# Retention and a token/channel mixer on one core: first-front tiles in either group of PSUM banks, and k of two batches cast unscaled by the DMA queue

## The chip, the cores and the metric

The kernel runs on one core of a Trainium2 chip. The metric is the device time of one execution in microseconds (us). The core has TensorE (PE in the profile; its weight loads are a row of their own, PEld), VectorE (DVE), ScalarE (ACT), GpSimd (POOL) and SyncE (SP). Transfers are issued by SP and by POOL; in this kernel those that change the data type on the way are issued by POOL. Matrix products land in PSUM, of which the kernel uses eight banks of 128 x 512 numbers of 32 bits.

## The reference

Inputs q, k, v have the shape (4 batches, 8 heads, 768 steps, 64). The first half is retention with a decay for each head, the second a mixer over the 768 steps and then over the 512 channels:

```
gamma = 1.0 - 2.0 ** (-5.0 - np.arange(H))
for t in range(S):
    state = gamma * state + einsum('bhd,bhe->bhde', k[:, :, t], v[:, :, t])
    y[:, :, t] = einsum('bhd,bhde->bhe', q[:, :, t], state) / sqrt(D)
x  = y with the heads laid side by side                      # (4, 768, 512)
h  = relu(x^T @ w_tok1) @ w_tok2                             # tokens: 768 -> 256 -> 768
u  = x + h^T
out = u + relu(u @ w_ch1) @ w_ch2                            # channels: 512 -> 1536 -> 512
```

All inputs and the output are of 32 bits; the products are made from operands of 16 bits (f16).

## The kernel before, in words

**Tiling.** The 768 steps are cut into six chunks of 128 and the eight heads into four pairs. For each batch there is a `front` of four pairs (`front(b, p)`: retention and token mixing) and a `back` (`back(b)`: channel mixing). Within a chunk retention is a masked product of scores with v; between chunks it is a state per head, carried with the decay to the power 128.

**The decay.** `gk` holds the decay to the minus step for each head, a number for each partition; `gy` the matching factor of the output. Line 317 multiplies k by `gk` while it turns it from f32 into f16 (`k16`, two VectorE instructions for a pair). Everything that uses k, the scores as well as the states, uses this scaled tile.

**One pair of a front, in order.** Loads of k (into `kf`, 32 bits, line 261), q (line 283 in batch 0, 280 in batch 1) and v (line 286). In batches 0 and 1 POOL issues them, and q and v are cast to f16 on the way; only the k of batch 0's pair 0 comes by SP. Batches 2 and 3 come by SP as 32 bits, and POOL casts q and v (line 298). Then: the scaling (317); the transposes of k and q on TensorE into a PSUM tile (333 and 337) and their copies out (345, VectorE for k and ScalarE for q in batch 0, ScalarE for both in batch 1), while batches 2 and 3 turn k and q by transposing transfers of SP (352); the sums of k and v of each chunk (366) and the running states `U` (375, 378), copied to `r` by ScalarE (385) and VectorE (392); the scores (408); their mask (421 on VectorE, or, for six tiles of batch 0 named in `ASIDE`, a plain copy by ScalarE at 419 and a cut by POOL at 425); the output y (442, 445), scaled into x (456, 460, 473); then the token mixing: product with w_tok1 (496), relu (504), product with w_tok2 (517), addition to x (524), f16 copy (535) and the turn of u into `uT` (548 and 557 in batch 0, a transfer of SP at 571 later).

**Back.** `ch1` (line 604) multiplies `uT` by w_ch1, 12 tiles for each half of the steps, with relu at 617; `ch2` (637) multiplies by w_ch2, adds x (646), and SP stores (653).

**PSUM.** Each temporary is a `Slot` with a tag; `BUFS` says how many buffers a tag has. The eight banks are `fa=5` for the fronts and `ba=3` for the backs; in batch 0 the token mixing of pairs 0 and 1 (`TOKBA = 2`) uses `ba` too.

**Order.** The program of each engine is written out in the order that a planner (`arrange`) finds. Every step is an `Op` with its engine, a rank (`prio`), the time for which it holds its engine (`occ`), a latency, its dependences and the slots that it takes and uses. The planner keeps a clock for each engine, lets a slot be taken when the users of the buffer's last holder have ended, and picks the step that can start first, by rank within 20 ns. Transfers have modelled durations on two rings, SP's and POOL's. POOL's transfers of batches 0 and 1 and of the weights are chained in one order (`queue`): for pair p of batch 0 k, q, v, then behind pair 3 w_tok1, w_tok2 (line 207) and w_ch1 in two pieces, then batch 1, with w_ch2 behind its pair 1. While batch 0's front has gaps, TensorE is given products with zeros (line 198), as many as the planned gap holds.

Of the kernel before, what the change touches and what calls it, by code (L numbers as in the profile page):

```python
# [13 lines left out]
ALU = mybir.AluOpType  # L14
# [3 lines left out]
def kernel(  # L18
# [11 lines left out]
    nc = tc.nc  # L30
# [53 lines left out]
    for t in r16:  # L84
# [8 lines left out]

    BUFS = dict(kf=4, qf=4, vf=4, k16=3, q16=4, v16=4, kT=4, qT=4, U=3, am=8, x16=2, h1=4, u16=3, u16w=2,
                x=3, uT=3, h2=2, o=3, r16=NR, fa=5, ba=3)
    SEM, GUARD = 80, 100
    EARLY, LATE, DIRECT = 1000, 12, 3
    LONG, XK, XQ, XU, XBAR = 1, 2, 2, 1, 1200
    RING = dict(SP=3, POOL=6)
    QLONG = 1200  # L100
    ASIDE, RACT = ((1, 1), (1, 3), (2, 1), (2, 3), (3, 1), (3, 3)), ()
    KPOOL = ()
    FILL, TOKBA, PRE, TWICE, SOFT = 0.75, 2, 2, 1, 2
    ops = []

    class Slot:


        def __init__(self, tag):
            self.tag, self.users, self.tile = tag, [], None  # L110

# [11 lines left out]
    def arrange():  # L123


        way = {}
        for op in reversed(ops):
            if op.first is not None:
                way[op] = way.get(op, 0) + op.lat + SEM
                for d in op.deps:  # L130
                    way[d] = max(way.get(d, 0), way[op])
        for op in ops:
            if op.first is not None:
                op.prio = (op.prio[0], 0, EARLY * op.first - way[op], op.first)
        free = dict(PE=5700, ACT=5000, DVE=4600, POOL=1100, SP=1300, SPring=1300, POOLring=1300)
        taken = {t: [] for t in BUFS}
        todo, order, ring = list(ops), [], dict(SP=[], POOL=[])
        while todo:
            best = []
            for op in todo:  # L140
                if any(d.end is None for d in op.deps):
                    continue
                start = free[op.eng]
                if op.dma and len(ring[op.eng]) >= RING[op.eng]:
                    start = max(start, ring[op.eng][op.count - 1 - RING[op.eng]])
                for d in op.deps:
                    if d.eng == op.eng and (d.dma or d.eng == "PE"):
                        continue
                    start = max(start, d.end + (30 if d.eng == op.eng else SEM) + op.guard)
                more = {}  # L150
                for s in op.takes:
                    q = taken[s.tag]
                    n = len(q) + more.get(s.tag, 0) - BUFS[s.tag]
                    more[s.tag] = more.get(s.tag, 0) + 1
                    if n >= 0:
                        old = q[n]
                        if any(u.end is None for u in old.users):
                            break
                        start = max([start] + [u.end + SEM for u in old.users])
                else:  # L160
                    best.append((start, op))
            t = min(b[0] for b in best)

            eng = min(best, key=lambda b: (b[0], b[1].prio))[1].eng
            start, op = min((b for b in best if b[1].eng == eng and b[0] <= t + 20),
                            key=lambda b: b[1].prio)
            free[op.eng] = start + op.occ
            op.start = start
            if op.dma:

                mine, other = op.eng + "ring", ("POOL" if op.eng == "SP" else "SP") + "ring"
                at = max(free[mine], start + (op.occ + 200 if op.eng == "POOL" else 50))
                both = max(0, free[other] - at)
                shared = min(op.dma, both // 2)
                if op.eng == "SP" and at > 5000:

                    at, shared = max(at, free[other]), 0
                free[mine] = at + op.dma + shared
                free[other] += shared
                op.end = free[mine] + 1600  # L180
                ring[op.eng] += [op.end if op.eng == "POOL" else free[mine]] * op.count
            else:
                op.end = start + op.lat
            for s in op.takes:
                taken[s.tag].append(s)
            todo.remove(op)
            order.append(op)
        return order
# [33 lines left out]
    def front(b, p):  # L222
        first = b == 0
        g = 0 if first else GUARD
        n = [0]

# [18 lines left out]
        srcs = dict(k=(k, Slot("kf")), q=(q, Slot("qf")), v=(v, Slot("vf")))  # L245
        KF = srcs["k"][1]

# [25 lines left out]
        def cast(slot, nm):  # L273
# [51 lines left out]
        def turn(src, dst, dep, eng):  # L325
            T = Slot("fa")

            def emit():
                T.tile = tp = tile_of(T, ps, [P, 512], FP).bitcast(F16)
                for c in range(NC):  # L330
                    if src is Q and soft and b < LONG:
                        for j in range(2):
                            nc.tensor.transpose(tp[j * D:(j + 1) * D, c * P:(c + 1) * P],
                                                src.tile[:, j * NC + c], ident16)
                        continue
                    o = src.tile[:, c] if src is K else src.tile[:, 2 * c:2 * c + 2]
                    nc.tensor.transpose(tp[:, c * P:(c + 1) * P], o.rearrange("p h d -> p (h d)"), ident16)  # L337
# [11 lines left out]
        def crossbar(src, dst, dep):  # L349
# [48 lines left out]
        for hf in range(2):  # L398
            A = [Slot("fa"), Slot("fa")]

# [10 lines left out]
            for j in range(2):  # L411
                off = first and (p, 2 * hf + j) in ASIDE
                M = AM[2 * hf + j]

                def emit(j=j, A=A, off=off, M=M):
# [16 lines left out]
        for hf in range(2):  # L432
            Y = Slot("fa")

# [53 lines left out]

        FA = "ba" if first and p < TOKBA else "fa"
        T1, H1 = Slot(FA), Slot("h1")  # L490

# [15 lines left out]
        wide = b >= XU  # L507
        T, UW = Slot(FA), Slot("u16w")
        for hf in range(2):
            T2, U16 = Slot(FA), UW if wide else Slot("u16")  # L510

# [28 lines left out]
            if first:  # L540
                T = Slot(FA)

# [168 lines left out]
```

## Time and profile before

| | |
|---|---|
| runs of the kernel before, median of 4 | 202.25 us (201.62 to 203.26) |
| the profiled execution | 201.41 us |
| its span in the profile | 199.7 us |
| granted TensorE clock | 0.998 |
| stand-in products, line 198, "fa" / "ba" | 37 and 3 instructions, 10.8 and 0.8 us |
| queue 0 (POOL's), packets and bytes | 25248, 9.83 MB |
| k loads issued by POOL | 7, 384.0 KB each, median 9.0 us to landing |
| v loads issued by POOL | 8, 192.0 KB each, median 7.4 us to landing |

The profile is one execution. A row of a chain or of a timeline begins with its start and its length in us, then engine, tile and line; a row of groups gives the busy time, the mean of one instruction in ns, and the idle time in front of it with what ended it. Of a transfer the answers give the time from the start of its issue to its landing. KB counts the bytes of the destination. The matrix products are pipelined, so that TensorE's busy share is not its share of peak. Time in which an engine that is not the bound stands idle costs nothing.

### The profile page before, as it was taken

The page shows a single profiled execution, that of the slowest core. Times are in us where ns is not written, and L with a number is a line of the kernel's source. Part 1 is how long each engine was busy: PE and PEld are TensorE (multiplying, and loading weights), DVE is VectorE, ACT ScalarE, POOL GpSimd, SP SyncE. Part 2 cuts the span into 40 slices and gives each one's busy share as a digit, 9 for nine tenths or more (in the row PEclk, how much of TensorE's full clock was granted, in tenths as well). Part 3 has the DMA queues.
Part 4 walks back from the last instruction along what each step waited for, and adds up shares of the span by engine and source line. Part 5 has one row for each costly group of instructions (what it writes and reads, how often), then busy time and mean ns, then how long its engine had stood idle before and what let it go on. Part 6 is the DMA issues. An engine that isn't in the chain of part 4 may idle for free.

```text
span 199.7 us, 4693 instructions
## 1 busy us (share of the span) xinstructions
PE 190.9 (96%) x1876; PEld 117.3 (59%) x1876; DVE 112.2 (56%) x285; ACT 92.3 (46%) x207; POOL 77.3 (39%) x124
## 2 busy tenths in 40 slices
PE   7698999999999999899999999999999999999993
PEld 2454796667766555666566755665666545545552
DVE  6599766585479675755786387628772021021021
ACT  7265996886682111275216530563326405504600
POOL 7997899944603531233534333343131000000000
PEclk9999999999999999999999999999999999999999
DMA  7999999999999989999999998999614021012012
GB/s 116 182 216 185 208 226 196 153 186 213 158 137 221 222 187 138 253 268 150 220 211 266 247 193 201 233 234 176 96 54 116 18 88 70 3 53 105 0 53 105
DMA packets 90069, 31.75 MB, mean 159 GB/s; under 512 B 82592, under 2 KB 85920, under 8 KB 90048
## 3 DMA queue, kind: packets, MB, share of 16 engines
q1 hardware_dynamic: 64800, 21.63, 55.8%
q0 software_dynamic: 25248, 9.83, 42.7%
q8 instruction: 14, 0.23, 0.5%
q14 instruction: 7, 0.06, 0.1%
HBM read 26.74 MB, written 6.29 MB: 165 GB/s over the span
## 4 chain that ended last, share of the span: by engine, by line
PE 79%; DMA 9%; POOL 6%; DVE 2%; issue 1%; SPq 1%; POOLq 0%; DVEq 0%
PE ba L637 30%; PE ba L604 28%; DMA wt<-in_moe_w_tok_dram 5%; PE fa L496 4%; PE fa L517 4%; PE fa L408 3%; DMA vf<-in_v_dram 3%; PE fa L445 2%; POOL v L286 2%; PE fa L442 2%; POOL kf L261 2%; PE fa L366 2%; PE fa L337 1%; DMA qT<-q 1%; POOL q L283 1%
## 5 line engine op out<-in xcount | busy, mean ns | idle before, releaser
L604 PE MATMUL ba<-uT,wc 128*128 128x384 f16 x384 | 69.2, 326 | 0.0
L637 PE MATMUL ba<-wc,h 128*128 128x512 f16 (+1 forms) x300 | 68.1, 371 | 0.0
L617 ACT ACTIVATE h<-ba 128x384 f16<-128x384 f32 x96 | 46.8, 492 | 38.4 <-PE ba L604 37.9
L604 PEld LDWEIGHTS <-wc 128*128 128x128 f16 x384 | 35.4, 98 | 22.1
L637 PEld LDWEIGHTS <-h 128*128 128x128 f16 x300 | 27.6, 98 | 25.8
L646 DVE TENSOR_TENSOR o<-x,ba 128x512 f32<-128x512 f32 (+1 forms) x25 | 16.6, 663 | 41.0 <-PE ba L637 41.0
L421 DVE TENSOR_TENSOR am<-fa,mask 128x384 f16<-128x384 f32 x58 | 30.0, 550 | 3.4 <-PE fa L408 2.8
L473 POOL CAST x<-x 128x384 f16<-128x384 f32 x30 | 15.2, 511 | 29.2 <-issue 19.3
L456 ACT ACTIVATE x<-fa,gy 128x192 f32<-128x192 f32 (+1 forms) x42 | 15.0, 424 | 15.7 <-PE fa L445 15.7
L524 DVE TENSOR_TENSOR x<-x,fa 128x384 f32<-128x384 f32 x28 | 14.7, 550 | 12.3 <-PE fa L517 12.1
L535 POOL CAST u16w<-x 128x384 f16<-128x384 f32 x24 | 11.9, 507 | 24.0 <-DVE x L524 23.7
L378 DVE SCALAR_TENSOR_TENSOR U<-U,gp,fa 128x64 f32<-128x64 f32 x64 | 17.7, 277 | 1.3
L317 DVE TENSOR_SCALAR k<-kf,gk 128x384 f16<-128x384 f32 x32 | 13.7, 470 | 4.5 <-DMA kf<-in_k_dram 4.5
L385 ACT ACTIVATE r<-U 64x320 f16<-64x320 f32 x16 | 7.5, 466 | 16.9 <-DVE U L378 16.9
L504 ACT ACTIVATE h<-fa 128x256 f16<-128x256 f32 x14 | 5.4, 386 | 20.8 <-PE fa L496 20.8
L445 PEld LDWEIGHTS <-am 128*128 128x128 f16 x192 | 12.2, 98 | 2.9
L445 PE MATMUL fa<-v,am 128*128 128x64 f16 x192 | 13.6, 193 | 0.0
L517 PEld LDWEIGHTS <-wt 128*128 128x128 f16 x192 | 11.9, 98 | 2.6 <-issue 0.2
L198 PE MATMUL fa<-zero 128*128 128x512 f16 x37 | 10.8, 428 | 2.5 <-DVE zero L52 1.3
L496 PEld LDWEIGHTS <-wt 128*128 128x128 f16 x192 | 11.7, 98 | 2.4 <-DMA wt<-in_moe_w_tok_dram 0.4
L442 PE MATMUL fa<-r,qT 128*128 128x128 f16 x80 | 12.1, 220 | 0.0
L517 PE MATMUL fa<-h,wt 128*128 128x128 f16 x168 | 12.0, 219 | 0.0
(61 smaller groups left out, 171.1 us busy)
## 6 DMA issues: line engine op xcount, KB each, us to landing
out_dram<-o SPq DMA_DIRECT2D x23, 256.0 KB, 2.6
kf<-in_k_dram SPq DMA_DIRECT2D x9, 384.0 KB, 5.2
qf<-in_q_dram SPq DMA_DIRECT2D x8, 384.0 KB, 5.2
vf<-in_v_dram SPq DMA_DIRECT2D x8, 384.0 KB, 5.5
kf<-in_k_dram POOLq DMA_DIRECT2D x7, 384.0 KB, 9.0
v<-in_v_dram POOLq DMA_DIRECT2D x8, 192.0 KB, 7.4
wc<-in_moe_w_ch_dram POOLq DMA_DIRECT2D x1, 1536.0 KB, 13.3
wc<-in_moe_w_ch_dram POOLq DMA_DIRECT2D x1, 1024.0 KB, 13.6
```

Source lines behind the costliest of these rows:

```text
L378: nc.vector.scalar_tensor_tensor(U[:, c], U[:, c - 1], gp[:, p:p + 1], o, ALU.mult, ALU.add)
L421: nc.vector.tensor_tensor(am, src[:, :HC], mask, ALU.mult)
L442: nc.tensor.matmul(o, QT.tile[:, c * P:(c + 1) * P], R[:, c - 1], start=True, stop=False)
L445: nc.tensor.matmul(o[:, j * D:(j + 1) * D], AM[2 * hf + j].tile[:, i], V.tile[:, j * NC + c], start=(c == 0), stop=(c == 0 or j == 1))
L456: nc.scalar.mul(dst[:, :, j * D:(j + 1) * D], yv[:, :, j * D:(j + 1) * D], gy[:, h:h + 1])
L473: nc.gpsimd.tensor_copy(X16.tile[:, half(hf)], X.tile[:, half(hf), pc])
L496: nc.tensor.matmul(acc[:, jt * P:(jt + 1) * P], wt1[:, i, jt * P:(jt + 1) * P], X16.tile[:, i], start=(i == 0), stop=(i == NC - 1))
L517: nc.tensor.matmul(acc[:, i * P:(i + 1) * P], wt2[:, jt, t], H1.tile[:, jt], start=(jt == 0), stop=(jt == NJ - 1))
L604: nc.tensor.matmul(acc[:, :SH], w[:, ct, f * P:(f + 1) * P], UT.tile[:, ct, sh * SH:(sh + 1) * SH], start=(ct == 0), stop=(ct == NP - 1))
L617: nc.scalar.activation(H2.tile[:, ft], A.tile[:, :SH], AF.Relu)
L637: nc.tensor.matmul(A.tile[:, :CW], H2.tile[:, ft, i * P:(i + 1) * P], wc2[:, ft, cs], start=(ft == 0), stop=(ft == NF - 1))
L646: nc.vector.tensor_tensor(o[:, :CW], X.tile[:, sh * HC + i, cs], A.tile[:, :CW], ALU.add)
```

## The change

It has four parts.

1. In batch 0 a front's PSUM slots (turns, states, scores, y; all four pairs, `FREE = 4`) may be taken from "fa" or "ba", whichever the planner finds free first; the token mixing of pairs 0 and 1, so far only in "ba", likewise.
2. The k of batches 0 and 1, but for the first pair, is cast to f16 by POOL's transfer, unscaled, into a new tile `kr` (four buffers; `kf` has three instead of four). The turn of k reads this tile and depends on its landing. Since `kr` has heads before chunks, the turn makes 12 transposes of 64 columns in place of 6 of 128.
3. The scaled copy `k16` (line 317's instructions) is made from `kr` and is used only by the states. The factor `gk` comes into the scores with the mask: a three-operand instruction on VectorE, or a multiply instead of a copy on ScalarE for the six tiles of `ASIDE`.
4. The planner: the scaling of a cast k counts 400 instead of 900 ns. SP's transfers no longer wait in the model for all of POOL's ring, but only for POOL transfers of more than 1900 ns, and share the rest.

The diff, cut to what is spoken of:

```diff
-    BUFS = dict(kf=4, qf=4, vf=4, k16=3, ...
+    BUFS = dict(kf=3, qf=4, kr=4, vf=4, k16=3, ...
-    LONG, XK, XQ, XU, XBAR = 1, 2, 2, 1, 1200
+    RAW, KOCC, LONG, XK, XQ, XU, XBAR = 1, 400, 1, 2, 2, 1, 1200
-    FILL, TOKBA, PRE, TWICE, SOFT = 0.75, 2, 2, 1, 2
+    FREE, FILL, TOKBA, PRE, TWICE, SOFT = 4, 0.75, 2, 2, 1, 2
...
-        def __init__(self, tag):
-            self.tag, self.users, self.tile = tag, [], None
+        def __init__(self, *choice):
+            self.choice, self.tag, self.users, self.tile = choice, None, [], None
...
                 for s in op.takes:
-                    q = taken[s.tag]
-                    n = len(q) + more.get(s.tag, 0) - BUFS[s.tag]
...
+                    when = []
+                    for tag in s.choice:
+                        n = len(taken[tag]) + more.get(tag, 0) - BUFS[tag]
+                        if n < 0:
+                            when.append((0, len(when), tag))
+                        elif all(u.end is not None for u in taken[tag][n].users):
+                            when.append((max(u.end + SEM for u in taken[tag][n].users), len(when), tag))
+                    if not when:
+                        break
+                    at, _, tag = min(when)
+                    start = max(start, at)
...
+                if op.eng == "SP" and at > 5000:
+                    for t0, t1 in long:
+                        if at + op.dma > t0:
+                            at = max(at, t1)
                 both = max(0, free[other] - at)
                 shared = min(op.dma, both // 2)
-                if op.eng == "SP" and at > 5000:
-                    at, shared = max(at, free[other]), 0
                 free[mine] = at + op.dma + shared
                 free[other] += shared
+                if op.eng == "POOL" and op.dma > 1900:
+                    long.append((at, free[mine]))
...
+        FB = ("fa", "ba") if first and p < FREE else ("fa",)
+        FT = ("fa", "ba") if first and p < TOKBA else ("fa",)
...
-        KF = srcs["k"][1]
+        raw = soft and (b or p) and RAW
+        KF = Slot("kr") if raw else srcs["k"][1]
...
-        kl = load("k")
+        kl = cast(KF, "k") if raw else load("k")
...
-        kc = op(keng, 900, 980, emit, [kl, kdone[-1] if b else None], [K], [KF])
+        kc = op(keng, *((KOCC, KOCC + 80) if raw else (900, 980)), emit, [kl, kdone[-1] if b else None], [K], [KF])
...
-            T = Slot("fa")
+            T = Slot(*FB)
...
-                    if src is Q and soft and b < LONG:
+                    if src is KF or src is Q and soft and b < LONG:
                         for j in range(2):
                             nc.tensor.transpose(tp[j * D:(j + 1) * D, c * P:(c + 1) * P],
                                                 src.tile[:, j * NC + c], ident16)
...
-        kt = crossbar(K, KT, kc) if b >= XK else turn(K, KT, kc, "DVE" if first else "ACT")
+        if b >= XK:
+            kt = crossbar(K, KT, kc)
+        else:
+            kt = turn(KF if raw else K, KT, kl if raw else kc, "DVE" if first else "ACT")
...
-        ST, US, RS = Slot("fa"), Slot("U"), Slot("r16")
+        ST, US, RS = Slot(*FB), Slot("U"), Slot("r16")
...
-            A = [Slot("fa"), Slot("fa")]
+            A = [Slot(*FB), Slot(*FB)]
...
-                    if off:
+                    if off and raw:
+                        nc.scalar.mul(am, src[:, :HC], g)
+                    elif off:
                         nc.scalar.copy(am, src[:, :HC])
+                    elif raw:
+                        nc.vector.scalar_tensor_tensor(am, src[:, :HC], g, mask, ALU.mult, ALU.mult)
                     else:
                         nc.vector.tensor_tensor(am, src[:, :HC], mask, ALU.mult)
...
-            Y = Slot("fa")
+            Y = Slot(*FB)
...
-        FA = "ba" if first and p < TOKBA else "fa"
-        T1, H1 = Slot(FA), Slot("h1")
+        T1, H1 = Slot(*FT), Slot("h1")
...
-        T, UW = Slot(FA), Slot("u16w")
+        T, UW = Slot(*FT), Slot("u16w")
```

More of the change, by code (lines that the diff above doesn't have):

```diff
@@ L91 @@
     wc2 = const_p.tile([P, NF, C], F16, name="wc2")
-    BUFS = dict(kf=4, qf=4, vf=4, k16=3, q16=4, v16=4, kT=4, qT=4, U=3, am=8, x16=2, h1=4, u16=3, u16w=2,
+    BUFS = dict(kf=3, qf=4, kr=4, vf=4, k16=3, q16=4, v16=4, kT=4, qT=4, U=3, am=8, x16=2, h1=4, u16=3, u16w=2,
                 x=3, uT=3, h2=2, o=3, r16=NR, fa=5, ba=3)
@@ L137, in arrange @@
         todo, order, ring = list(ops), [], dict(SP=[], POOL=[])
+        long = []
         while todo:
@@ L150, in arrange @@
                 more = {}
+                op.tags = []
                 for s in op.takes:
-                    q = taken[s.tag]
-                    n = len(q) + more.get(s.tag, 0) - BUFS[s.tag]
[L154 to L159, printed above, removed]
+                    when = []
[9 more added lines that the diff above has]
+                    start = max(start, at)
+                    more[tag] = more.get(tag, 0) + 1
+                    op.tags.append(tag)
                 else:
@@ L183, in arrange @@
                 op.end = start + op.lat
-            for s in op.takes:
+            for s, s.tag in zip(op.takes, op.tags):
                 taken[s.tag].append(s)
@@ L413, in front, with emit @@
                 M = AM[2 * hf + j]
-                def emit(j=j, A=A, off=off, M=M):
+                def emit(j=j, A=A, off=off, M=M, g=gk[:, 2 * p + j:2 * p + j + 1]):
                     am = tile_of(M, sb, [P, HC, P], F16)
                     src = A[j].tile.rearrange("p (i t) -> p i t", t=P)
-                    if off:
+                    if off and raw:
+                        nc.scalar.mul(am, src[:, :HC], g)
+                    elif off:
                         nc.scalar.copy(am, src[:, :HC])
+                    elif raw:
+                        nc.vector.scalar_tensor_tensor(am, src[:, :HC], g, mask, ALU.mult, ALU.mult)
                     else:
@@ L507, in front @@
         wide = b >= XU
-        T, UW = Slot(FA), Slot("u16w")
+        T, UW = Slot(*FT), Slot("u16w")
         for hf in range(2):
-            T2, U16 = Slot(FA), UW if wide else Slot("u16")
+            T2, U16 = Slot(*FT), UW if wide else Slot("u16")
             def emit(hf=hf, T2=T2):
@@ L540, in front @@
             if first:
-                T = Slot(FA)
+                T = Slot(*FT)
             def emit(hf=hf, U16=U16, T=T):
```

## The prediction

> **What bounds the kernel now.** I read the page's engine totals first, then the chain that ended last in order of time, then the busy time by window, then the single transfers of the queue.
>
> The engine totals of the page (busy us, share of the span, instructions):
>
> ```profile
> PE 190.9 (96%) x1876; PEld 117.3 (59%) x1876; DVE 112.2 (56%) x285; ACT 92.3 (46%) x207; POOL 77.3 (39%) x124
> ```
>
> TensorE is the bound, but not all of its 190.9 us is work: the stand-in multiplications of line 198 with zeros take 11.6 us (37 in "fa" 10.8, 3 in "ba" 0.8). So 179.3 us are useful, and 199.7 - 179.3 = 20.4 us of the span are not. The question is where those lie. The chain says (start us, us, what):
>
> ```profile
> 11.98 0.99 POOL v L286
> 12.97 9.35 DMA wt<-in_moe_w_tok_dram
> 22.37 0.84 PE ba L496 x12
> 23.21 0.44 PE fa L408 x12
> 23.65 0.75 PE ba L198 x3
> ...
> 33.30 1.46 PE ba L604 x9
> ```
>
> Up to 12.97 the chain is POOL issuing transfers one after another; then it waits 9.35 us for the first token weight (wt1); from 22.37 on it is TensorE nearly to the end. The transfer's start is not what counts, since it stands in a queue: 9.35 us is its issue, the wait behind earlier transfers, and its own time. The busy time by window (columns: length, PE, PEld, DVE, ACT, POOL, then clock, DMA, GB/s) shows the rest:
>
> ```profile
> 7.20:13.00 5.80, 4.67 (x74) 3.02 (x73) 5.12 (x15) 1.93 (x3) 5.80 (x8) 1.00 1.51 206
> 13.00:23.00 10.00, 8.85 (x136) 5.68 (x132) 9.12 (x26) 7.43 (x16) 8.14 (x13) 1.00 1.59 197
> 23.00:33.40 10.40, 10.07 (x164) 8.31 (x162) 6.60 (x13) 9.27 (x27) 9.63 (x18) 1.00 1.42 214
> ```
>
> TensorE's column looks full, but most of line 198 lies here. DVE is at 91% from 13 to 23 and POOL at 93% from 23 on. After 33.4 there is one hole (80 to 92, 0.7 us idle) and the tail. So what this change can give must come out of the time before 33.3, and its gain is how much earlier the steady stretch of line 604 begins.
>
> **The change, part by part.**
>
> **(1) Seven k loads become casts (batch 0 pairs 1 to 3, batch 1).** The POOL issues stay seven, at 1.05 us each (line 261, median), against 1.04 for a casting v (line 286): POOL gains nothing. What changes is the time in the queue. Each transfer's landing is its issue start plus its time to landing. From the answers on single transfers:
>
> ```profile
> v<-in_v_dram POOLq DMA_DIRECT2D x1, 192.0 KB, 5.4
> kf<-in_k_dram POOLq DMA_DIRECT2D x1, 384.0 KB, 6.1
> ...
> v<-in_v_dram POOLq DMA_DIRECT2D x1, 192.0 KB, 6.5
> kf<-in_k_dram POOLq DMA_DIRECT2D x1, 384.0 KB, 7.3
> ```
>
> The v of pair 1 lands at 6.21 + 5.4 = 11.61, the k of pair 2 at 7.24 + 6.1 = 13.34: this k took 1.73. The v of pair 2 lands at 8.99 + 6.5 = 15.49, the k of pair 3 at 10.00 + 7.3 = 17.30: 1.81. The k of pair 1 by the same reckoning 1.63. Mean 1.72. The v behind each q: 1.40, 1.34 and 1.14, mean 1.29. A cast k has a v's shape (same runs read, same runs written), so each saves 0.43 us. Three stand ahead of wt1: 1.3 us, so wt1 lands near 21.0; all seven save 3.0 by the end of POOL's queue. A rule speaks against this: the Trainium skill, DMA: Bandwidth & Descriptors, section "Why small descriptors are slow", has a fixed cost for each packet beside the cost of its bytes; taken to its end, short runs are paid by the run and not by the byte. A cast leaves the runs read as they were and halves those written, from 256 to 128 bytes; paid by the run it saves nothing, and the sum loses its 1.3. The rows above decide for me: v has as many runs as k and takes less. Bounds 0 and 1.8 (three times the widest gap, 1.73 - 1.14); taken 1.3.
>
> **(2) k is turned before it is scaled.** The turn now follows the landing, not line 317, of which a pair takes 0.74 (4.69, 9.86) to 1.06 us (13.85). The turn makes 12 transposes of 64 columns in place of 6 of 128. The rows for both forms: line 333 (12 of them) holds TensorE 0.53, line 337 (6) 0.50. Seven turns: +0.2 us at most, taken 0, hidden in the stand-ins for batch 0 and, for batch 1, paid if at all.
>
> **(3) The scaled copy reads f16.** Line 317 takes 414 ns (median) from f32; no row has f16 in and out on VectorE. Two rules pull apart here. The Trainium skill, VectorE: DVE Perf Modes, "The perf-mode tier table", lets a 16-bit copy run at four elements a cycle in place of two: 384 x (1/2 - 1/4) / 0.96 = 100 ns less, an estimate, so 314; by it batch 0's six copies save 0.6 us. But SBUF — State Buffer, "Who interferes with whom", says that such two-port modes and GpSimd lock each other out. The trace agrees: pairs of line 317 take 0.74 us in some places and 1.00 to 1.10 where POOL is issuing transfers (13.85, 18.09, 33.57). With POOL at 81% (13 to 23) the block stays whatever the copy's own length. Bounds 0 and 0.6; taken 0.3 for batch 0. It is no longer ahead of the turn, but still ahead of the states (line 366).
>
> **(4) The mask also multiplies by the decay.** 6 masks of batch 0 and 16 of batch 1 become the three-operand form. Its price by rows: that form on 64 elements (line 378) 277 ns, a copy of 64 (line 375) 223, so 54 more than 550: 604. Batch 0 +0.3 us, batch 1 +0.9. With (3) batch 0's VectorE time is unchanged. In batch 1's time VectorE is busy 22.2 of 33 us (20 to 53) and 19.3 of 27 (53 to 80), by further windows; nothing of it shows, and if that cover were gone it would be 0.9. The six masks on ACT change from copy to multiply: 485 ns (line 419) against 492 for the activation of the same size (line 617): nothing.
>
> **(5) The first front may take eight banks.** This is where a stall goes. Pair 1's q landed at 4.91 + 5.3 = 10.2, its turn ran at 11.59; pair 3's landed at 19.1, its turn at 20.34, the copy of qT then at 21.27 while ACT had been idle 1.77 us before 20.29. TensorE's row of line 198 waiting on DVE am L421 (0.7 us) is such a bank. What is late next is VectorE: from 13 to 23 it has 10.00 - 9.12 = 0.88 us left, so pairs 1 to 3 cannot all come much earlier. What can be won after wt1 is what TensorE there does not need: 0.75 of stand-ins in the chain above, and the scores of pair 3 (lines 408, 0.44 + 0.27), which now stand between the first and second token multiplication and could run before wt1. Bounds 0 and 1.5. I take 0.8, about what VectorE's remaining room allows.
>
> **(6) The planner.** Costs and the model of SP's transfers change, so the order on all engines may. Nothing is added, but SP's queue is strict, and no row tells the new order. Bounds: -0.7 (the hole from 80 to 92 closes) to the rival below; taken 0. Batch 1's data arrives up to 3.0 us earlier against 2.1 for TensorE, so it keeps up.
>
> **Sum:** 1.3 + 0.8 = 2.1 us. The profiled execution took 201.41 (span 199.7 and 1.7 around it): 199.3. Its time stands 0.84 below the median 202.25, so for the median **200.1 us**.
>
> **The rivals.**
> **The queue is paid by the run** (the change doesn't do what it says): wt1 lands at 22.3 as before, and only the banks count: 202.25 - 0.8 = 201.4. For it speaks that the runs are short; against it the landings of v.
> **VectorE and POOL hold the front:** wt1 comes earlier, but pair 1's x, whose masks pass POOL at 18.87 to 19.93, and the pairs behind are not ready: TensorE gains some half of 1.3, 201.6. For it: 91% and 93% above. Against: the banks move just those steps.
> **More than that:** both upper bounds, 1.8 + 1.5 = 3.3, with the hole's 0.7: 198.2.
> **SP's strict queue turns against it (slower).** Place: 77 to 91, where the chain leaves TensorE:
>
> ```profile
> 77.46 2.77 DMA qT<-q
> ...
> 83.29 1.19 SPq L653
> 84.53 5.93 DMA vf<-in_v_dram
> ```
>
> TensorE's cover is used up there (0.7 us idle). If the new order puts one load of batch 2 behind a store that waits, TensorE stands. SP waited 44.5 us in 13 such waits (line 653 for line 646), mean 3.4, longest 10.0. One mean wait: 202.25 - 2.1 + 3.4 = 203.6; the longest 210. From 2.1 us of it the gain is gone, from 4.1 it is slower by over 1%. Against it: these waits are themselves for TensorE's products, and move earlier with it.
>
> **How the numbers follow.** About 1% (2 us) is what a measurement of this kernel can tell from no change. Forecast case (199.0 to 201.2) 0.45, of which I count 0.30 beyond 1%; both hidden cases together 0.22, within; more than that 0.12, faster; SP's queue 0.21, of which 0.18 over 1% slower, the mean wait being near the edge and the tail long. Faster 0.42, same 0.40, slower 0.18. The forecast case's own range is 199.0 to 201.2; the range that holds 8 in 10 goes from 198.2 (both upper bounds) to 203.6 (one mean wait).
>
> **What would show it.** Right: wt1 lands near 21.0 and line 496 starts there; stand-ins after it are gone; line 604's steady stretch begins near 31.2 instead of 33.3 and everything behind is shifted by about the same. (1) is wrong if the gap of a cast k is 1.7; (3) if line 317 still takes 414; (4) if the mask is far from 604; (5) if the q turns of pairs 1 and 3 still start over 1 us after landing. The forecast is wrong if TensorE shows new idle time between 50 and 140.

## The result, and the profile after

The changed kernel takes 201.41 us (median of 44 runs, 200.67 to 203.01). In the pooled runs the kernel before takes 201.91 us (63 runs). The ratio is 0.9986, with a 95% interval of 0.9972 to 0.9999: 0.3 us faster, where the prediction's sum said 2.1. That is within the 1% (2 us) which the prediction took as the least that can be told from no change. All ratios below are of fast executions, to those of the kernel before that ran beside them, so that a ratio and a quotient of medians can differ.

The profiled execution of the changed kernel took 202.24 us, span 200.5. In this execution one early transfer, the v of pair 0, landed 1.0 us later than in the profile of before (8.87 against 7.86), and the front behind it is later too. The kernel `banks_cast` below has the same casts, and in its profile this v lands at 7.86 again; where a place in time matters, that profile is read beside this one.

The engine totals of the changed kernel:

```profile
PE 191.1 (95%) x1906; PEld 115.9 (58%) x1906; DVE 113.0 (56%) x285; ACT 93.3 (47%) x207; POOL 76.7 (38%) x124
```

Nearly the same sums, with 30 more products: 42 transposes were added and 12 stand-ins fell away. The stand-ins (now line 210) still hold 10.0 us, 8.2 in "fa" and 1.8 in "ba", against 11.6. So TensorE's own products take 181.1 us, where they took 179.3. The busy time by window (length, PE, PEld, DVE, ACT, POOL, then clock, DMA, GB/s):

```profile
7.20:13.00 5.80, 4.33 (x67) 2.24 (x64) 4.25 (x12) 1.99 (x2) 5.80 (x8) 1.00 2.04 158
13.00:23.00 10.00, 8.38 (x153) 5.50 (x152) 9.63 (x28) 8.19 (x18) 7.43 (x12) 1.00 1.76 186
23.00:33.40 10.40, 8.96 (x154) 7.84 (x151) 7.35 (x17) 8.89 (x26) 9.91 (x18) 1.00 1.64 190
```

DVE went from 9.12 to 9.63 of 10 us in the middle window. In the last one PE lost busy time, 10.07 to 8.96: it waits there, and stand-ins do not fill it. Which work is it waiting for? The queue did what step (1) said. Single transfers of the changed kernel, time from issue to landing last:

```profile
v<-in_v_dram POOLq DMA_DIRECT2D x1, 192.0 KB, 6.2
kr<-in_k_dram POOLq DMA_DIRECT2D x1, 192.0 KB, 6.4
q<-in_q_dram POOLq DMA_DIRECT2D x1, 192.0 KB, 6.5
...
wt<-in_moe_w_tok_dram POOLq DMA_DIRECT2D x1, 384.0 KB, 9.2
```

The v of pair 1 lands at 6.20 + 6.2 = 12.40, the cast k of pair 2 at 7.23 + 6.4 = 13.63: this k took 1.23, where it took 1.73. From the landing of the v of pair 0 to that of wt1 it is now 21.93 - 8.87 = 13.06 us, before 22.27 - 7.86 = 14.41: 1.35 less, against the 1.3 of the sum. But the chain of waits does not pass through that transfer any more. Chain of the changed kernel in its front (start us, us, what):

```profile
9.27 0.24 DVE U L395
...
10.28 1.05 DVE k L334 x2
...
20.59 0.47 ACT r L405
21.06 0.47 ACT am L439
21.52 1.34 ACT qT L362
...
25.55 0.53 POOL am L449
...
28.43 0.53 POOL u L558
...
29.34 0.67 PE fa L519 x12
...
33.19 0.49 PE ba L627 x3
...
33.85 1.95 PE ba L627 x12
```

From 9.27 to 20.57 the chain is VectorE alone, piece on piece, then ScalarE until 25.55, then POOL until 28.96. No landing stands in it after the v of pair 0. Line 519, the product with wt1, starts at 23.55, 1.6 us after its weight is there. The steady stretch of the channel product, behind the last turn of u, began at 33.30 before (line 604). It begins at 33.85 here and at 32.89 in banks_cast, not near 31.2.

Further on the hole from 80 to 92 is gone. Where the chain of before left TensorE at 77, 83 and 84, the changed kernel's has

```profile
76.29 1.83 PE ba L660 x8
78.41 0.86 PE ba L660 x4
79.61 1.73 PE ba L660 x8
```

and TensorE is busy for all 48.00 us from 92 to 140, as it was before. So new standing behind the front is not what took the gain.

The prediction's subtraction, span less TensorE's own products, can be carried through by stretch. In the table (us, one profiled execution each) "own products" is the busy time less the stand-ins, and "lost before 34" is standing and stand-ins together, up to the end of batch 0's front:

| kernel | own products | lost before 34 | lost 34 to 140 | lost from 140 | span |
|---|---|---|---|---|---|
| before | 179.3 | 16.4 | 0.8 | 3.2 | 199.7 |
| `banks_only` (below) | 179.7 | 16.0 | 0.0 | 3.2 | 198.8 |
| `banks_cast` (below) | 180.6 | 15.5 | 0.0 | 3.3 | 199.4 |
| the changed kernel | 181.1 | 16.2 | 0.0 | 3.2 | 200.5 |

Four kernels whose products are those of the kernel before (before, banks_only, and model_only and no_wt1 below) read 179.3 to 180.3 in the first column, so half a microsecond there says nothing. In banks_cast, without the late v, the front loses 0.9 us less and the hole is closed (0.8), but TensorE's own products grow by 1.3, which takes most of it back. The experiments show what holds the front, and that the turns of k are the larger part of what grew.

### The profile page after: what moved, and what is told of

Read it like the earlier page. It is cut to its first block, busy times and chain, and to the rows that moved or that the text cites. A ratio compares the mean times of both kernels' runs of the same rounds, so it can differ in the third digit from the quotient of the medians.

```text
span 200.5 us, 4748 instructions
## 1 busy us (share of the span) xinstructions
PE 191.1 (95%) x1906; PEld 115.9 (58%) x1906; DVE 113.0 (56%) x285; ACT 93.3 (47%) x207; POOL 76.7 (38%) x124
## 3 DMA queue, kind: packets, MB, share of 16 engines
q0 software_dynamic: 35328, 8.46, 44.9%
## 4 chain that ended last, share of the span: by engine, by line
PE 84%; DVE 6%; DMA 3%; ACT 2%; POOL 2%; issue 1%; POOLq 0%
PE ba L627 32%; PE ba L660 32%; PE fa L540 5%; PE fa L519 4%; DMA v<-in_v_dram 3%; PE fa L428 3%; PE fa L469 2%; PE fa L386 2%; PE fa L466 2%; DVE U L398 1%; DVE k L334 1%; DVE am L445 1%; PE fa L350 1%; PE fa L354 1%; ACT am L439 1%
## 5 line engine op out<-in xcount | busy, mean ns | idle before, releaser
L669 DVE TENSOR_TENSOR o<-x,ba 128x512 f32<-128x512 f32 (+1 forms) x25 | 16.6, 662 | 42.3 <-PE ba L660 42.0
L497 POOL CAST x<-x 128x384 f16<-128x384 f32 x30 | 15.5, 519 | 42.1 <-issue 24.0
L547 DVE TENSOR_TENSOR x<-x,fa 128x384 f32<-128x384 f32 x31 | 16.1, 549 | 12.3 <-PE fa L540 9.7
L445 DVE TENSOR_TENSOR am<-fa,mask 128x384 f16<-128x384 f32 x34 | 17.3, 549 | 4.3 <-PE fa L428 4.2
L480 ACT ACTIVATE x<-fa,gy 128x192 f32<-128x192 f32 (+1 forms) x32 | 11.7, 419 | 16.7 <-PE fa L469 16.5
L398 DVE SCALAR_TENSOR_TENSOR U<-U,gp,fa 128x64 f32<-128x64 f32 x60 | 16.5, 276 | 1.2
L540 PE MATMUL fa<-h,wt 128*128 128x128 f16 x186 | 13.2, 219 | 0.0
L519 PE MATMUL fa<-x,wt 128*128 128x128 f16 x180 | 12.5, 219 | 0.0
L469 PE MATMUL fa<-v,am 128*128 128x64 f16 x168 | 12.3, 193 | 0.0
L443 DVE SCALAR_TENSOR_TENSOR am<-fa,gk,mask 128x384 f16<-128x384 f32 x20 | 11.9, 609 | 0.1
L466 PE MATMUL fa<-r,qT 128*128 128x128 f16 x70 | 10.8, 220 | 1.1 <-DVE r L412 1.1
```

The costliest lines, as they stand in the source:

```text
L398: nc.vector.scalar_tensor_tensor(U[:, c], U[:, c - 1], gp[:, p:p + 1], o, ALU.mult, ALU.add)
L466: nc.tensor.matmul(o, QT.tile[:, c * P:(c + 1) * P], R[:, c - 1], start=True, stop=False)
L469: nc.tensor.matmul(o[:, j * D:(j + 1) * D], AM[2 * hf + j].tile[:, i], V.tile[:, j * NC + c], start=(c == 0), stop=(c == 0 or j == 1))
L497: nc.gpsimd.tensor_copy(X16.tile[:, half(hf)], X.tile[:, half(hf), pc])
L519: nc.tensor.matmul(acc[:, jt * P:(jt + 1) * P], wt1[:, i, jt * P:(jt + 1) * P], X16.tile[:, i], start=(i == 0), stop=(i == NC - 1))
L540: nc.tensor.matmul(acc[:, i * P:(i + 1) * P], wt2[:, jt, t], H1.tile[:, jt], start=(jt == 0), stop=(jt == NJ - 1))
```

## The experiments

All ratios are to the kernel before, 95% interval in brackets.

### Which half of the change moves the time

The parts are switched on alone or in pairs. Parts 2 and 3, and with them the 400 ns of part 4, are one switch, `RAW`; banks_only, cast_only and banks_cast have the planner's old model of transfers.

```diff
 # banks_only: shared banks (FREE = 4), k as before
-    RAW = 1
+    RAW = 0
 # cast_only: cast k, the front on its five banks
-    FREE = 4
+    FREE = 0
-        FT = ("fa", "ba") if first and p < TOKBA else ("fa",)
+        FT = ("ba",) if first and p < TOKBA else ("fa",)
 # model_only: neither, only the planner's new model of SP's transfers
 # banks_cast: both, with the planner's old model
```

> The kernel before with one part of the change: the first front's PSUM tiles may lie in either group of banks; k loaded as 32 bits and the planner's model of transfers as before. By the prediction 0.8 us shorter than before (0 to 1.5), with fewer stand-ins and the turns of q sooner after their landing. By the rival that VectorE, ScalarE and POOL hold the front: the turns are sooner, but the steady stretch of the channel product begins within 0.3 us of 33.3 and the time is within 0.3 us of before.

> The kernel before with one part of the change: k of batches 0 and 1 cast unscaled by the queue, decay with the mask, scaled copy for the states; banks and the planner's model of transfers as before. By the prediction wt1 lands near 21.0 and the time is 1.3 us shorter. By the rival that the queue is paid by the run, wt1 lands near 22.3 and the time is within 0.3 us. If the first cast k holds up the v in front of it (landing near 8.9 instead of 7.9), VectorE's states start 1 us later and the time is the same or up to 1 us longer.

> The kernel before with only the planner's model of SP's transfers changed, so only the order of instructions differs, from batch 1 on. By the prediction 0. If the order is what gave the gain back, 0.5 us or more longer than before; if it is what gave the little gain there is, 0.3 to 0.7 shorter.

> The changed kernel with the planner's model of transfers put back: banks and cast together. By the prediction 2.1 us shorter than before. If the front is held by VectorE, ScalarE and POOL, between 0 and 0.7 shorter. Beside the whole change this tells what the model is worth with the other two: nothing by the prediction.

| run | ratio | median us |
|---|---|---|
| banks_only | 0.9929 [0.9906, 0.9953] | 200.69 |
| cast_only | 1.0124 [1.0075, 1.0174] | 204.76 |
| model_only | 1.0017 [0.9994, 1.0041] | 202.32 |
| banks_cast | 0.9975 [0.9956, 0.9995] | 201.26 |

The banks alone are worth 1.4 us (0.0071 x 202), nearly the upper bound of step (5). Not all of it lies where step (5) put it. In the profiles the front loses 0.4 us less (16.4 and 16.0 in the table above), and the steady stretch begins at 32.97 in place of 33.30. More of it is the hole behind the front. TensorE's busy time from 60 to 92, before and then in banks_only:

```profile
60.00:92.00 32.00, 31.32 (x311) 18.94 (x308) 22.06 (x53) 9.90 (x25) 11.38 (x20) 1.00 1.18 210
60.00:92.00 32.00, 32.00 (x330) 19.23 (x328) 22.72 (x54) 12.51 (x28) 10.81 (x18) 1.00 1.08 207
```

These are single executions, so the shares are not exact. The planner's model is worth nothing that shows: in model_only's profile the hole is gone too (32.00), but 4.1 us are lost from 140 on in place of 3.2. The cast takes away from the banks instead of adding to them: with both, the gain falls from 0.71 to 0.25%. And alone it makes the kernel 1.2% slower, which none of the predicted parts explains; it is taken up last.

### Does the first token weight hold TensorE at all?

`no_wt1` is the kernel before with the transfer of wt1 left out, in the same order; `after_nowt1` is the changed kernel with the same edit.

```diff
+    for i in range(3):
+        nc.scalar.copy(wt1.rearrange("p i j -> p (i j)")[:, i * 512:(i + 1) * 512], zero)
...
+            if key == ("t1", 0):
+                return None
```

> The kernel before, same order of every engine, with the transfer of the first token weight left out (three copies of zeros on ScalarE at the start fill it, so the token mixing adds nothing to x). By the prediction's step 1 the end follows this weight's landing: with it there from the start the steady stretch moves by far more than 1.3 us, the more so as all later transfers land 2 us earlier. By the reading that TensorE waited only 0.33 us for it, the gain is at most that 0.3 to 0.5 us.

> The changed kernel in its own order, with the transfer of the first token weight left out (the tile is filled with zeros by three ScalarE copies at the start, so the token mixing adds nothing; all else is computed as before). If that transfer's landing (21.9 us in the profile of the changed kernel) held the front, as the prediction's step (1) has it, the time falls by over 1.3 us against the changed kernel, to about 0.992 of the kernel before. If VectorE, ScalarE and POOL hold it, by no more than 0.5 us: 0.996 to 0.9985.

`no_wt1`: 0.9964 [0.9941, 0.9988], so 0.7 us (0.2 to 1.2), though the weight is there from the start and the transfers behind it move up by about 2 us. `after_nowt1`: 0.9990 [0.9967, 1.0012] beside 0.9986 for the changed kernel itself: nothing. The reason stands in a view that the prediction did not show, the waits of TensorE. In the kernel before:

```profile
PE fa L366 <- DMA v<-in_v_dram: 0.5, 1, 0.5
...
PE ba L496 <- DMA wt<-in_moe_w_tok_dram: 0.3, 1, 0.3
```

TensorE stood 0.3 us for wt1, once. The chain's "12.97 9.35 DMA wt" is true, and is not a price: a chain names what came last, and TensorE was busy with the y of pair 1 until 22.04, 0.33 us before. In this order an earlier landing of wt1 can win no more than that before the next releaser takes its place; what no_wt1 wins beyond it may come from the later transfers. In banks_only's profile wt1 even lands later than before, at 12.94 + 10.1 = 23.04, and the span is 0.9 us shorter. In the changed kernel with the weight left out the waits are

```profile
PE ba L473 <- POOL am L453: 1.2, 1, 1.2
PE fa L470 <- DVE r L416: 1.2, 1, 1.2
```

and the chain runs through VectorE, ScalarE and POOL with the same pieces as above:

```profile
19.98 0.47 DVE kT L366
20.44 0.20 DVE U L402
20.66 0.47 ACT r L409
...
25.72 0.54 POOL am L453
...
33.36 0.49 PE ba L631 x3
```

The stretch begins at nearly the same place, with the weight and without it (33.19 and 33.36 for its first three products; the v of pair 0 is late in both profiles). In the order of the changed kernel the transfer is off the path. What a planner could make of a weight that is there from the start, these two runs do not show.

### What the cast costs in the changed kernel

Three pieces of work hang on the cast k: turns of 64 columns, the scaled copies, the decay in the masks. Two are new; copies of the same size, from f32, stood in the kernel before as well. Each piece is taken out of the changed kernel in its own order; `none_of_three` takes out all. These kernels do not compute the whole: wide_turns leaves columns of k in other places, no_copies leaves the decay out of the states, plain_masks leaves it out of the scores. What no_copies wins is thus a test of whether VectorE holds the front, and not a price of the cast.

```diff
 # wide_turns
-                    if src is KF or src is Q and soft and b < LONG:
+                    if src is Q and soft and b < LONG:
 # no_copies: the states read kr
+            if raw:
+                K.tile = KF.tile.rearrange("p (h c) d -> p c h d", h=2)
+                return
 # plain_masks
-                    if off and raw:
+                    if off and raw and False:
-                    elif raw:
+                    elif raw and False:
```

> The changed kernel in its own order, each turn of a cast k made as 6 transposes of 128 columns (wrong columns, same amount). By the prediction's step 2 nothing or 0.2 us. If the four turns of batch 1 are paid in full on a busy TensorE, 0.4 to 0.5 us shorter than the changed kernel.

> The changed kernel in its own order, the scaled copies left out (the states are made from the unscaled k, so their decay is missing). If the landing of wt1 set the first front, nothing; if VectorE's chain sets it (its chain from 9.3 to 20.6 holds three pairs of copies, 1.05, 0.66 and 0.71 us), 1 to 2 us shorter than the changed kernel.

> The changed kernel in its own order, the decay left out of the scores of the cast k: plain masks on VectorE and plain copies on ScalarE. By the prediction's step 4 the masks cost nothing (0.3 us of VectorE in the first front, hidden): the time of the changed kernel. If ScalarE and VectorE hold the first front, six multiplies at about 0.58 in place of copies at 0.485 and six masks at 0.61 in place of 0.55 give 0.3 to 0.9 us back.

> The changed kernel in its own order with all three left out: plain masks, turns of 128 columns, no scaled copies. This is what remains of the cast when it costs no engine anything. By the prediction about 0.5 us shorter than the changed kernel. If the engines' steps are where the gain went, 1.5 to 3 us shorter, and below banks_only (0.993 of before).

| run | ratio | against the changed kernel, 0.9986 |
|---|---|---|
| wide_turns | 0.9935 [0.9913, 0.9957] | -0.51%, 1.0 us |
| no_copies | 0.9883 [0.9834, 0.9933] | -1.03%, 2.1 us |
| plain_masks | 0.9986 [0.9965, 1.0008] | 0 |
| none_of_three | 0.9831 [0.9783, 0.9878] | -1.55%, 3.1 us |

The sizes are those of ratios. The medians (201.32 for wide_turns, 200.20 for no_copies, 199.31 for none_of_three, against 201.41) give 0.1, 1.2 and 2.1 us. The 0.1 is a median between two groups: 10 of 22 executions of wide_turns lie at 200.5 to 200.7, where the changed kernel has 2 of 44. I take the order of the three as shown, their sizes to about half.

**The turns.** In batch 1 the chain of the changed kernel holds both forms, the turn of k (line 350) and that of q (line 354):

```profile
35.80 0.46 PE fa L350 x12
...
37.66 0.34 PE fa L354 x6
...
60.21 0.46 PE fa L350 x12
60.67 0.44 PE fa L354 x6
```

A turn of k takes 0.12 us more than one of q, where products stand between them. Where the turn of q follows at once, as in two of batch 1's four pairs, the two take 0.90; in wide_turns the chain has one row at that place, "59.67 0.67 PE fa L354 x12". So it is 0.23 more there, and 2 x 0.12 + 2 x 0.23 = 0.7 us for batch 1. The two chains agree: from the start of the steady stretch to the end of batch 1's last turn it is 33.85 to 61.11 in the changed kernel and 33.75 to 60.34 in wide_turns, 0.67 us less. It is paid in full, since TensorE is busy for all 26.00 us from 34 to 60.

**The copies.** The two forms in the changed kernel (ns min/median/max):

```profile
L334 DVE TENSOR_SCALAR k<-kf,gk x18: 400/413/971, 4.7 to 134.1; 128x384 f16<-128x384 f32 x18
L334 DVE TENSOR_SCALAR k<-kr,gk x14: 301/318/911, 10.2 to 57.7; 128x384 f16<-128x384 f16 x14
```

318 against an estimate of 314: the rule of the Trainium skill, VectorE: DVE Perf Modes, "The perf-mode tier table", held. The maximum of 911 goes with the other rule that the prediction weighed, SBUF — State Buffer, "Who interferes with whom", in direction: a pair of these copies takes 0.54 us at 57.51, where POOL does nothing, 0.79 beside POOL's own casts (18.92, 32.60, 50.89), and 0.96 and 1.13 where it issues transfers without a gap (39.90, 10.20). For the f32 form of before the prediction's "the trace agrees" was too quick: its pairs at 9.86 and 38.12 took 0.74 although POOL was issuing there as well (8.99 to 11.24 and 37.49 to 39.28).

Batch 0's three pairs take 1.05 + 0.66 + 0.71 = 2.4 us of the VectorE chain above. Leaving them out gives back about half of that, so VectorE is what holds this stretch until another engine takes over. With the copies gone the chain ends

```profile
30.99 0.49 PE ba L630 x3
31.48 0.17 PE fa L574 x3
31.64 1.95 PE ba L630 x12
```

so the steady stretch starts at 31.64: 2.2 us earlier than in the changed kernel's profile with its late v, and 1.25 earlier than in banks_cast (32.89).

**The masks.** Both forms are slower than what they replace, and the time does not show it (groups of the changed kernel: busy us, mean ns, idle before):

```profile
L443 DVE SCALAR_TENSOR_TENSOR am<-fa,gk,mask 128x384 f16<-128x384 f32 x20 | 11.9, 609 | 0.1
...
L439 ACT ACTIVATE am<-fa,gk 128x384 f16<-128x384 f32 x4 | 2.3, 583 | 0.5 <-PE fa L428 0.5
```

609 on VectorE against 604 predicted; 583 on ScalarE, where the prediction took 492.

### Scaling before the turn, and one batch at a time

`cast_scaled` casts k in the transfer but scales it before it is turned, as the kernel before did, with plain masks. `cast_b0` and `cast_b1` have the cast, turn and masks of the change in one batch only. All three have the banks and the old planner model.

```diff
 # cast_scaled
-            kt = turn(KF if raw else K, KT, kl if raw else kc, "DVE" if first else "ACT")
+            kt = turn(K, KT, kc, "DVE" if first else "ACT")
 # ... and the masks as in plain_masks
 # cast_b0
-        raw = soft and (b or p) and RAW
+        raw = first and p and RAW
 # cast_b1
-        raw = soft and (b or p) and RAW
+        raw = b == 1 and RAW
```

> Banks shared, k of batches 0 and 1 cast by the queue, but scaled before the turn as in the kernel before: turns of 128 columns from the scaled copy, plain mask, plain copies on ScalarE. Only the transfer's type and the copy's source type differ from banks_only. If the cast itself costs nothing and the cost lies in what comes with an unscaled k (64-column transposes, multiplying masks), this is within 0.3 us of banks_only or faster, near 200.5. If the cast transfers or the copies from f16 are the cost, it is near banks_cast, about 0.9 us above banks_only.

> Banks shared, unscaled cast k in batch 0 only (three pairs). Against banks_only: if the cost of the cast lies in the first front (ScalarE's masks 0.1 us each longer, six of them; VectorE's three-operand masks), it is 0.5 to 0.9 us above banks_only; if it lies in the dense stretch, within 0.3.

> Banks shared, unscaled cast k in batch 1 only (four pairs). Here TensorE is full: four turns of 12 transposes take 0.44 to 0.46 in place of 0.34 us, so 0.4 to 0.5 us above banks_only; if only the first front pays, within 0.2 of banks_only.

Measured: 0.9956 [0.9930, 0.9981], 0.9925 [0.9901, 0.9948] and 0.9937 [0.9910, 0.9963]. None is better than the banks alone (0.9929) by more than the intervals. cast_scaled lies between its two expectations, and tells nothing. The cast in batch 0 costs nothing that shows and brings nothing; in both batches it costs 0.46%. cast_b1 was expected 0.4 to 0.5 us above the banks alone: it is 0.2 by the ratios and 0.6 by the medians (201.26 and 200.69), within the intervals of either. The two batches do not add up, since the planner finds a new order for each of these kernels; how much of the 0.46% is the order and how much the four turns of batch 1 (0.7 us, 0.33%) these runs do not separate. `cast_b0` and `banks_only` are the fastest versions that compute the whole, 0.7% below the kernel before and faster than the changed one.

### Why the cast alone is slower

`cast_only_wide` and `cast_only_none` are cast_only in its own order, with wide turns, and with all three pieces out.

```diff
 # cast_only_wide
-                    if src is KF or src is Q and soft and b < LONG:
+                    if src is Q and soft and b < LONG:
 # cast_only_none: this, the copies and the masks as above
```

> The cast without the shared banks, in the order of cast_only, with the turn of k made of 6 transposes of 128 columns in place of 12 of 64 (its columns are then in the wrong places; the time is what is looked at). If the turns cost here what they cost in the changed kernel, 0.7 to 1.0 us: 1.007 to 1.009 of the kernel before. If the turns are most of the 2.5 us that cast_only lost, because on five banks each turn delays the next, near 1.000 to 1.003.

> The cast without the shared banks, in the order of cast_only, with wide turns, without the scaled copies and without the decay in the masks (so the decay is missing from scores and states). If the three additions cost here what they cost with the banks shared (1.55%, 3.1 us), 0.997 of the kernel before, so that the queue's gain is worth some 0.6 us and the loss of cast_only is these additions. If the order itself, with five banks, is what loses, the time stays above 1.003.

Measured: 1.0125 [1.0087, 1.0163] and 1.0151 [1.0114, 1.0188]. Taking out the three pieces, worth 1.55% with the banks shared, wins nothing here. So they are not the cause. What is left is the order that the planner finds for five banks with this queue, and the casting transfers themselves, with their 1440 packets more each; these runs do not separate the two. The waits of TensorE in cast_only_none say where:

```profile
PE fa L385 <- DMA v<-in_v_dram: 1.5, 2, 1.2
PE fa L206 <- ACT qT L361: 1.3, 2, 0.7
...
PE fa L427 <- DMA qT<-q: 1.1, 1, 1.1
```

Part is the front, where the next turn waits for a bank that a copy still reads (line 206, the stand-ins in front of a turn, for ACT). More of it is later: by the subtraction above cast_only_none loses 16.6 us before 34 and 3.0 from 34 to 140 (before: 16.4 and 0.8), in stretches where the kernel before has hardly a gap:

```profile
59.98 0.35 PE L385 MATMUL fa<-v,kr 128*64 128x64 f16 x10 [1.16 <-DMA v<-in_v_dram]
79.59 0.51 PE L427 MATMUL fa<-qT,kT 64*128 64x128 f16 x12 [1.09 <-DMA qT<-q]
```

The first is batch 1's last v, issued at 51.01 and landed 8.9 us later, while SP loads batch 2 (the same transfer took 6.0 in the profile of cast_only). The second is batch 2's q. cast_only_wide shows such waits too (0.9 for a v that POOL casts, at 120.85, and 0.9 for qT). The third expectation of cast_only, that the first cast k holds up the v in front of it, did not come: that v landed at 2.87 + 4.8 = 7.67. The second stands at the place that the prediction's slower rival named (77 to 91), TensorE without data of batch 2, but in another kernel than the one it was meant for; and the chain leads from it to SP's loads at 54 to 61 us, not to a load behind a waiting store. What cannot be said: the profiled execution of cast_only itself took 202.68, the shortest of its six, and has none of these waits, so that for its median of 204.76 there is only the evidence of its two relatives.

## Why the prediction was wrong, by its own steps

| step | taken | measured |
|---|---|---|
| (1) casts shorten POOL's queue | 1.3 gain | the landing 1.35 earlier; worth 0 (after_nowt1) |
| (2) turns of 64 columns | 0 | loss: 0.7 in batch 1 by the rows, 1.0 by the ratio of wide_turns |
| (3), (4) copies and masks | 0 on VectorE together | cast with wide turns (0.9935) is as fast as no cast (0.9929): 0 |
| (5) eight banks | 0.8 gain | 1.4 gain with all that the new order brings; by the profiles 0.4 in the front and 0.8 in the hole |
| (6) planner | 0 | 0 (model_only) |
| sum | 2.1 gain | 1.4 less 0.7 to 1.0: 0.4 to 0.7; the change 0.3, banks_cast 0.5 |

**Step (1), the one that failed.** "Three stand ahead of wt1: 1.3 us, so wt1 lands near 21.0" came true but for the late v; in banks_cast, whose profile has no such v, it landed at 12.73 + 8.2 = 20.93. What failed is what the sum then made of it: that a weight which lands 1.3 us earlier ends the front 1.3 us earlier. TensorE had stood 0.33 us for it. What held the front in its place was the chain through VectorE (to 20.57), ScalarE (to 25.55) and POOL (to 28.96). The rival "VectorE and POOL hold the front" had this mechanism, and with 201.6 nearly the time; the evidence for it was in the window rows that the prediction itself showed (91 and 93%). The argument against it, "the banks move just those steps", was true of the banks and said nothing of the queue. The rival also missed ScalarE, which has the chain for 5 us. The queue is not without a part in every order: in banks_only's profile the chain does go through a landing, that of pair 3's k ("10.01 9.32 DMA kf"). But in banks_cast this k lands at 9.98 + 6.4 = 16.38 in place of 19.33, and the time is no shorter.

**Step (1)'s rule** (the Trainium skill, DMA: Bandwidth & Descriptors, "Why small descriptors are slow"). Its fixed cost was taken to its end, payment by the run alone, and that did not hold: k's gap fell by 0.40 to 0.50. Something of a fixed cost may show in the q behind each k of pairs 1 and 2, which took longer, 0.72 and 0.81 before, 1.11 and 1.10 now; the q behind the k of pair 3 took less, 1.82 and 1.50. The queue's packets rose while its megabytes fell:

```profile
q0 software_dynamic: 35328, 8.46, 44.9%
```

25248 packets before, 9.83 MB: (35328 - 25248) / 7 = 1440 more for each cast k. The three casts in front of wt1 still brought 1.35 us.

**Step (2)** read "line 333 (12) holds TensorE 0.53, line 337 (6) 0.50". Those are lengths of single groups, from the first start to the last modelled end, with the whole of the last product in it (0.22 us). What a group costs on a full engine is the step to the next group, and that is 0.46 against 0.34, or 0.90 against 0.67 for a k and a q in a row. This is the second step that failed: 0.2 us at most, taken 0, was 0.7.

**Steps (3) and (4)** had the right durations on VectorE (on ScalarE the mask took 0.1 us more than the 492 ns, which no run shows in the time). Put together as "VectorE's time is unchanged" they were also the reason why nothing could be gained in the front by an earlier k: an engine that is 91% busy before and has the same work after ends at much the same time.

**Step (5)** was right in kind, but that its total came near the upper bound of 1.5 is in part luck. In the front the banks won about 0.4, less than the 0.8 taken; the rest is the hole, which step (6) had named and left out of the sum. By the step's own sign it came half true: the q turn of pair 1, which began 1.4 us after its landing before, begins at once in the changed kernel (landing 11.21, turn 11.22), but that of pair 3 still waits 1.7 us (18.78 and 20.45; before 1.2).

**Steady stretch** near 31.2, in place of 33.30: it came at 33.85 in this profile, and at 32.89 in that of banks_cast. "New idle time between 50 and 140" did not come in the changed kernel.

## What to carry to other kernels

A long row in the chain of waits says who came last, not what its absence would bring: before a transfer's gain is counted, look up in the bound engine's own waits how long it stood for it, and who comes next. When the chain of a stretch runs through several engines that are each over 90% busy, a change gains there only by what it takes off that chain; here the cast moved work from one of them to another, and added to the engine that is full later. A gain in the total can come from another place than the one that the argument names: look for the place. What an added instruction costs on the bound engine is its step to the next one, not its length.

## What was not expected of the hardware

- One early transfer, the v of pair 0, issued at 2.9 us in each of these kernels, takes up to 1.6 us longer in one profile than in another: "2.87 5.98 DMA v" in the chain of the changed kernel, 5.05 for the same transfer in cast_only_none, 6.2 in after_nowt1, 4.6 in no_copies. The times of the changed kernel fall in two groups, about 201.3 and 202.3, and its profiled execution, with the late v, is of the second. That the late v makes the second group is not shown, since one execution of each kernel was traced. Medians of few runs can be off by as much.
- A casting load with half the bytes written had 1440 packets more and still took 0.5 us less (1.23 against 1.73).
- ScalarE's activation from PSUM with a scale for each partition took 583 ns, its plain cast of the same tile 485.
